# Row sums of the unit before the last: by ACT from the first score product, or by ones on TensorE

## The chip, the cores and the metric

The kernel runs on one core of one Trainium2 chip. The metric is the device time of one execution in microseconds (us). TensorE (PE, with its weight loads PEld), VectorE (DVE), ScalarE (ACT) and GpSimd (POOL) compute; SyncE (SP) issues almost all DMAs here.

## The reference, cut to what matters

A block of two parts over 2048 tokens of width 1024: an attention with a compressive memory (32 heads of width 32, four segments of 512 tokens, causal inside a segment), then an MLP. The change touches the softmax inside a segment:

```
logits = einsum("bhqd,bhkd->bhqk", qs, ks) * scale + mask
p      = softmax(logits, axis=-1)
a_dot  = einsum("bhqk,bhkd->bhqd", p, vs)
o      = g * a_mem + (1.0 - g) * a_dot
```

Afterwards `o @ wo` is added to the tokens, and layer norm, two dense layers with a GELU and a second addition follow. All in fp32; the dense products are made of three products of split operands (high x high, low x high, high x low).

## The kernel before, in words

The tokens are worked in two halves of 1024 tokens, each of two segments. In a half the attention runs over 16 **units**: eight groups `g` of four heads, and in each group the two segments `sl`. A unit's dense part (`dense`) projects keys, queries and values in 24 steps on TensorE, one step being one call of `mm3` (three matmuls). All that follows for the unit (`follow`) is written into a table of due times, in steps counted from the unit's start, and is performed between the dense steps of later units. So the score work of unit n lies beside the dense work of units n+1 and n+2. Behind the last unit the output product (`wo_first`) takes the place of the dense steps, with what is left of the table between its products. TensorE's order is the order of this table, fixed by hand; the order of the other engines comes from a scheduler with a cost model, with the dependences and buffers as limits.

What `follow` does for a unit, by the letters of the tables:

- `q` (`qk`, 16 calls: four heads, four row blocks): first score product into a bank of PSUM (`pqk`, one of four banks that the second product shares), then one DVE instruction (L663) that adds the mask, negates and gives the row maximum to `mx`. In an ordinary unit its output goes to an SBUF tile `sm` (four buffers), and ACT (L666) takes the exp of it only for the row sum, which goes to `mx` too.
- `x`, `y`, `z`: the maxima are split, transposed, and written over DRAM into two more rows of the query stack `qs`, so that the second product has the maximum already subtracted.
- `p` (`again`, 12 calls): second, transposed score product `psc`, exp by ACT into `pt` (L695), triangle by POOL (L697).
- `r`, `w` (`inverse`, `weigh`; ordinary units): reciprocal of the 16 columns of sums times the gate, a transpose `pw` on TensorE, a copy by ACT, a store to `r_dram` and four loads that spread it over `w`.
- `a`, `o` (`av`, `av_out`): product of `pt` with the values into `po`, times `w`, plus the memory part, then the split for the output product.

In the last group (`g == NG - 1`, so two units per half) `r` and `w` do nothing. L663 writes back into its PSUM bank and there is no exp for sums. Instead DVE adds the four `pt` blocks of a head (`sums`, L704 to L706), TensorE multiplies `pt` and the added block by `ones` (`den`, eight matmuls, in `av`), DVE takes the reciprocal of the whole 128x512 `den` (L739), and `av_out` has the gate as a per-row scalar.

The due times of the two last units differ from the ordinary ones: `LAST_FOLLOW` and `LAST_PACE` hold for the unit before the last, `END_FOLLOW` and `END_PACE` for the last. They have entries for `r` and `w` as well.

```
FOLLOW = dict(q=28.2, x=47.3, y=47.4, z=50.2, r=47.6, w=51.2, p=60.3, a=82.3, o=85.2)
PACE = dict(q=(4.7,1.2), p=(4.0, 1.3))
LAST_FOLLOW = dict(q=29.2, x=43.3, y=43.4, z=48.1, r=43.6, w=46.2, p=58.5, a=70.6, o=72.6)
LAST_PACE = dict(q=(3.5,0.9), p=(2.6,.85))
```

A pace `(a, b)` gives the steps from head to head and from block to block. The last unit's start is 24 steps behind that of the unit before it.

Of the kernel before, what the change touches and what calls it, by code (L numbers as in the profile page):

```python
# [10 lines left out]
F32 = mybir.dt.float32  # L11
# [6 lines left out]
P = 128  # L18
# [8 lines left out]
NG = 8  # L27
# [28 lines left out]
def build(tc, x, wq, wk, wv, wo, beta, w1, b1, w2, b2, out):  # L56
# [312 lines left out]
    def attention(half, first):  # L369
# [4 lines left out]
        def tmp(name):  # L374
            return ab.tile([P, 512], F32, tag="tmp", name=name, bufs=5)
# [262 lines left out]

        def follow(u):
            table, pace = (FOLLOW, PACE) if u["g"] < NG - 1 else ((LAST_FOLLOW, LAST_PACE), (END_FOLLOW, END_PACE))[u["s"] % 2]  # L640
            if u["g"] == NG - 1:
                for j in range(4):
                    u["at"](table["p"] + pace["p"][0] * j + LAG, partial(sums, u, j))
            for op, t in table.items():
                fn = fns[op]
                if op in pace:
                    a, b = pace[op]
                    for j in range(4):
                        for k, i in enumerate({"q": (0, 2, 1, 3), "p": (0, 1, 2)}[op]):
                            u["at"](t + a * j + b * k, partial(fn, u, j, i))  # L650
                else:
                    u["at"](t, partial(fn, u))

        def qk(u, j, i):
            if "mx" not in u:
                u["mx"] = ab.tile([P, 64], F32, name="mx", bufs=2)
            mx, n = u["mx"], P * (i + 1)
            pqk = psum.tile([P, 512], F32, tag="qk", name="pqk", bufs=4)
            one_small()
            nc.tensor.matmul(pqk[:, :n], u["qs"][0:96, j, i * P:(i + 1) * P], u["ks"][0:96, j, 0:n], start=True, stop=True)  # L660
            k = 4 * j + i
            pr = pqk if u["g"] == NG - 1 else ab.tile([P, 512], F32, name="sm", bufs=4)
            nc.vector.tensor_tensor_reduce(out=pr[:, :n], in0=pqk[:, :n], in1=mask[:, 512 - n:512], op0=ALU.add, op1=ALU.min,  # L663
                                           scale=-1.0, scalar=3.0e38, accum_out=mx[:, k:k + 1])
            if u["g"] < NG - 1:
                nc.scalar.activation(pr[:, :n], pr[:, :n], AF.Exp, bias=mx[:, k:k + 1], scale=-1.0, accum_out=mx[:, 16 + k:17 + k])  # L666

        def largest(u):
# [37 lines left out]
            SME.tensor_tensor(sm[:, 128:384], sm[:, 128:384], p2, op=ALU.add)  # L706

        def inverse(u):
            if u["g"] == NG - 1:
                return  # L710
            rs = u["rs"] = ab.tile([P, 32], F32, name="rs", bufs=2)
            nc.vector.reciprocal(rs[:, 0:16], u["mx"][:, 16:32])
            r4 = rs[:, 0:16].rearrange("p (h i) -> p h i", i=4)
            GTE.tensor_tensor(r4, r4, gate[:, 1, 4 * u["g"]:4 * u["g"] + 4].unsqueeze(2).to_broadcast([P, 4, 4]), op=ALU.mult)

        def weigh(u):
            n = acts["weighed"] = 1 - acts.get("weighed", 0)
            w = u["w"] = tmp("w") if u["g"] == NG - 1 and u["s"] % 2 else scr[n][:, 1]
            if u["g"] == NG - 1:
                return  # L720
            pw = ps_dense("pw")
            nc.tensor.transpose(pw[0:16, 0:P], u["rs"][:, 0:16], ident)
            nc.scalar.copy(w[0:16, 0:P], pw[0:16, 0:P])
            d = r_dram[n]
            BQ.dma_start(d, w[0:16, 0:P])
            for k in range(4):
                BQ.dma_start(w[32 * k:32 * k + 32, :],
                                  bass.AP(tensor=d.tensor, offset=d.offset + 512 * k, ap=[[0, DH], [1, 512]]))

        def av(u):  # L730
            u["po"] = psum.tile([P, 512], F32, tag="av", name="po", bufs=1)
            for jk in (0, 1, 3, 2):
                abreast([(u["po"][32 * j:32 * j + 32, P * jk:], u["v"]["vn"][:, j, jk, :], u["pt", jk][j], jk == 0, jk == 2)
                         for j in range(4)])
            if u["g"] == NG - 1:
                den = psum.tile([P, 512], F32, tag="qk", name="den", bufs=4)
                abreast([(den[32 * j:32 * j + 32, 0:P], ones, u["pt", 0][j][:, 0:P], True, True) for j in range(4)])
                abreast([(den[32 * j:32 * j + 32, P:], ones, u["sm"][j], True, True) for j in range(4)])
                nc.vector.reciprocal(u["w"], den)  # L739
            bursts()  # L740
# [5 lines left out]
        def av_out(u):  # L746
            w = u["w"]
            sl, g = u["s"] % 2, u["g"]
            home = w
            if kept(sl, g):  # L750
                if g % 2 == 0:
                    acts["home"] = {**acts.get("home", {}), sl: lnp.tile([P, D], F32, tag="ln", name="orr", bufs=4)}
                home = acts["orr", sl, g] = acts["home"][sl][:, 512 * (g % 2):512 * (g % 2) + 512]
            first = home if u["omt"] is None else w
            if g == NG - 1:
                nc.vector.scalar_tensor_tensor(w, u["po"], gcol, w, op0=ALU.mult, op1=ALU.mult)
            else:
                nc.vector.tensor_tensor(first, u["po"], w, op=ALU.mult)
            if u["omt"] is not None:
                w4, h4 = (t.rearrange("p (k c j) -> p k c j", k=4, c=4) for t in (w, home))  # L760
                nc.gpsimd.tensor_tensor(h4, w4, u["omt"].rearrange("p (c k j) -> p k c j", k=4, c=4), op=ALU.add)
            if u["g"] >= NG - 2:
                oh, ol = o_tiles(half, u["s"] % 2)
                split(None, w, oh[:, u["g"], :], ol[:, u["g"], :], hi_eng="scalar", lo_eng="vector")
            else:
                u["done"] = True
# [39 lines left out]
        prev = None  # L806
        for g in range(NG):
            for sl in range(2):
                u = {"g": g, "s": 2 * half + sl, "T": TIMES, "v": {}, "next": {}}
                d = dense(g, sl, ws, u)  # L810
                if prev is None:
                    interleave(d, acts.pop("ahead") if half else ln1(0, 1, aside=ws.pop("rest")), 1.1 if half else 1.6)
                    if first:
                        constants()
                    if "last" in acts:
                        acts.pop("last")
                else:
                    if g == NG - 1:
                        for n, fn in WO_AT[sl]:
                            acts["todo"].setdefault(acts["unit"] + 24 + n, []).append((0.9, n, fn))  # L820
                    with in_order(mybir.EngineType.PE, keep=False):
                        for _ in d:
                            pass
                prev = u
            ws = u["next"]
# [798 lines left out]
```

## Time and profile before

| | |
|---|---|
| median of 3 runs | 2139.03 us (2135.96 to 2140.15) |
| the profiled execution's own time | 2141.17 us |
| its span | 2139.5 us, 33505 instructions |
| TensorE busy | 2105.0 us, 98% |
| DVE, ACT, POOL busy | 1348.6 (63%), 1030.5 (48%), 853.9 us (40%) |
| DMA | 441.47 MB, mean 206 GB/s |

The shares are means over stages of quite different kinds. A view of waits names, for each group of instructions, what ended the idle time before it; a view in order of time gives start and duration of single instructions; "L666" is line 666 of the kernel. The last two units of the first half lie at about 364 to 414 us, those of the second at about 1159 to 1210 us; the output product follows each.

### The profile page before, as it was taken

The numbers are of one execution on the slowest core, as the hardware profiler recorded it, in microseconds if no ns is written. First come the engines' busy times: TensorE is split into PE (matmuls) and PEld (weight loads), VectorE is DVE, ScalarE is ACT, GpSimd is POOL, SyncE is SP. The second block draws the span as 40 slices with busy tenths as digits, with TensorE's granted clock in tenths as the row PEclk, the third lists the DMA queues.
The fourth block names the chain that finished last, engine by engine and source line by source line (L and its number), as shares of the span: only waits on it lengthen the run. The fifth ranks groups of instructions, "written<-read, shape, count | busy, mean of one in ns | idle before, by whom it ended". The sixth has DMA issues, their size and how long they took to land.

```text
span 2139.5 us, 33505 instructions
## 1 busy us (share of the span) xinstructions
PE 2105.0 (98%) x11157; PEld 1705.5 (80%) x11157; DVE 1348.6 (63%) x2679; ACT 1030.5 (48%) x2181; POOL 853.9 (40%) x937
## 2 busy tenths in 40 slices
PE   8999999999999999999999999999999999999999
PEld 6777877768888887877777778888888788888887
DVE  6666666676745556666666686655666675567653
ACT  5676677533633445667677434633443232323321
POOL 5333333432544423333333342534455544246340
PEclk9999999999999999999999999999999999999999
DMA  7777777834666557777778734665669774676762
GB/s 247 220 228 219 222 220 212 251 119 148 210 192 192 152 156 214 206 220 217 231 222 231 233 119 143 211 182 168 180 219 389 244 245 166 206 232 230 255 217 89
DMA packets 405783, 441.47 MB, mean 206 GB/s; under 512 B 36622, under 2 KB 270570, under 8 KB 405610
## 3 DMA queue, kind: packets, MB, share of 16 engines
q1 hardware_dynamic: 342442, 402.62, 60.9%
q10 hardware_dynamic: 63168, 36.71, 5.7%
q8 instruction: 88, 1.44, 0.3%
q14 instruction: 85, 0.70, 0.1%
HBM read 296.32 MB, written 142.90 MB: 205 GB/s over the span
## 4 chain that ended last, share of the span: by engine, by line
PE 88%; DMA 5%; DVE 3%; SPq 1%; POOL 1%; ACT 1%; issue 1%; ACTq 0%; POOLq 0%; DVEq 0%
PE po L1456 23%; PE bps L1060 10%; PE cps L1060 7%; PE dps L1060 7%; PE pqk L660 3%; PE psc L693 3%; PE po L463 3%; PE qps L140 3%; PE vps L140 3%; PE vps L141 3%; PE vps L142 3%; PE kps L140 3%; PE qps L141 2%; PE qps L142 2%; PE kps L141 2%; PE kps L142 2%
## 5 line engine op out<-in xcount | busy, mean ns | idle before, releaser
L663 DVE CUSTOM_DVE_ANT_0 sm<-pqk,mask 128x128 f32<-128x128 f32 x448 | 217.4, 488 | 205.5 <-PE pqk L660 194.4
L666 ACT ACTIVATE sm<-sm,mx 128x128 f32<-128x128 f32 x448 | 251.5, 562 | 175.3 <-DVE mx L663 172.5
L695 ACT ACTIVATE pt<-psc 128x512 f32<-128x512 f32 (+1 forms) x384 | 198.9, 521 | 94.6 <-PE psc L693 90.7
L697 POOL TENSOR_SCALAR_AFFINE_SELECT pt<-pt 128x128 f32<-128x128 f32 (+1 forms) x384 | 138.4, 366 | 253.8 <-ACT pt L695 250.6
L1466 DVE TENSOR_TENSOR c<-c,po 128x512 f32<-128x512 f32 x160 | 105.5, 684 | 154.5 <-PE po L1456 147.2
L660 PE MATMUL pqk<-ks,qs 96*128 96x128 f32 (+3 forms) x512 | 171.1, 335 | 11.9 <-DMA qs<-qs_dram 9.0
L693 PE MATMUL psc<-qs,ks 98*128 98x512 f32 (+3 forms) x512 | 139.5, 314 | 2.3 <-DVE mx L663 2.3
L1456 PE MATMUL po<-w2h,zh 128*128 128x512 f32 x378 | 120.9, 390 | 1.6 <-ACT zh L1395 1.2
L660 PEld LDWEIGHTS pqk<-ks,qs 96*128 96x128 f32 x512 | 96.6, 189 | 31.5 <-issue 9.4
L791 POOL TENSOR_TENSOR wl<-wr,wh 128x1024 fp32r<-128x1024 f32 x42 | 101.0, 2405 | 40.4 <-PE pqk L660 20.5
L693 PEld LDWEIGHTS psc<-qs,ks 98*128 98x128 f32 x512 | 95.9, 189 | 26.1 <-DVE mx L663 4.5
L1313 POOL TENSOR_TENSOR w2r<-w2r 128x512 f32<-128x512 f32 x54 | 84.6, 1576 | 72.8 <-DMA w2r<-in_B_w 50.2
L1060 PE MATMUL bps<-zh,sb 128*128 128x512 f32 x336 | 111.0, 391 | 0.0
L1060 PE MATMUL bps<-zh,sa 128*128 128x512 f32 x336 | 110.7, 390 | 0.0
L140 PE MATMUL kps<-yh,wh 128*128 128x512 f32 (+1 forms) x264 | 109.2, 414 | 0.0
L140 PE MATMUL qps<-yh,wh 128*128 128x512 f32 x256 | 107.8, 421 | 0.0
L140 PE MATMUL vps<-yh,wh 128*128 128x512 f32 x256 | 103.8, 405 | 0.0
L1456 PE MATMUL po<-w2h,hl 128*128 128x512 f32 x322 | 103.1, 390 | 0.4 <-DVE hl L1396 0.4
L141 PE MATMUL kps<-yl,wh 128*128 128x512 f32 (+1 forms) x264 | 102.9, 390 | 0.1
L142 PE MATMUL kps<-yh,wl 128*128 128x512 f32 (+1 forms) x264 | 102.5, 388 | 0.0
L1172 POOL TENSOR_TENSOR s<-r 128x512 f32<-128x512 f32 x28 | 44.1, 1574 | 142.8 <-DVE sa L1188 86.1
L141 PE MATMUL qps<-yl,wh 128*128 128x512 f32 x256 | 100.8, 394 | 0.0
(269 smaller groups left out, 5926.7 us busy)
## 6 DMA issues: line engine op xcount, KB each, us to landing
hr<-h_dram SPq DMA_DIRECT2D x112, 448.0 KB, 5.7
w2r<-in_B_w SPq DMA_DIRECT2D x122, 256.0 KB, 4.5
r<-in_B_w SPq DMA_DIRECT2D x56, 512.0 KB, 4.4
ks<-ks_dram SPq DMA_DIRECT2D x64, 384.0 KB, 3.9
qs<-qs_dram SPq DMA_DIRECT2D x64, 384.0 KB, 4.3
h_dram<-ht ACTq DMA_DIRECT2D x84, 256.0 KB, 3.6
ks_dram<-kh SPq DMA_DIRECT2D x64, 256.0 KB, 4.7
qs_dram<-qh SPq DMA_DIRECT2D x64, 256.0 KB, 3.0
```

What stands on the lines that cost most here:

```text
L140: nc.tensor.matmul(ps, ah, bh, start=first, stop=False)
L141: nc.tensor.matmul(ps, ah, bl, start=False, stop=False)
L142: acts["mm"] = nc.tensor.matmul(ps, al, bh, start=False, stop=last)
L660: nc.tensor.matmul(pqk[:, :n], u["qs"][0:96, j, i * P:(i + 1) * P], u["ks"][0:96, j, 0:n], start=True, stop=True)
L663: nc.vector.tensor_tensor_reduce(out=pr[:, :n], in0=pqk[:, :n], in1=mask[:, 512 - n:512], op0=ALU.add, op1=ALU.min, scale=-1.0, scalar=3.0 ...
L666: nc.scalar.activation(pr[:, :n], pr[:, :n], AF.Exp, bias=mx[:, k:k + 1], scale=-1.0, accum_out=mx[:, 16 + k:17 + k])
L693: nc.tensor.matmul(ps[:, o:o + m], u["ks"][:, j, jk * P:(jk + 1) * P], u["qs"][:, j, P * jk:], start=True, stop=True)
L695: nc.scalar.activation(pt, ps[:, :w], AF.Exp)
L697: nc.gpsimd.affine_select(d, d, pattern=[[1, P]] if len(groups[n]) == 1 else [[0, 2], [1, P]], compare_op=ALU.is_ge, fill=0.0, base=0, cha ...
L1060: nc.tensor.matmul(ps, x_[:, c, :], y_[:, c, :], start=first and c == 0 and n == 0, stop=last and c == 3 and n == 2, skip_group_check=True)
L1456: nc.tensor.matmul(ps, x_[:, k], y_[k], start=opens and k == 0 and i == 0, stop=closes and k == self.KP - 1 and i == 2, skip_group_check=True)
L1466: nc.vector.tensor_tensor(o, o, ps, op=ALU.subtract if name == "4" else ALU.add)
```

## The change

The ones on TensorE remain for one unit per half only, the last (`"last": g == NG - 1 and sl == 1`). The unit before it (`g == NG - 1`, `sl == 0`) does what the ordinary units do: L663 writes to `sm`, ACT makes the row sums with 16 exps, `inverse` and `weigh` do their work at the times that `LAST_FOLLOW` has for `r` and `w`, and `sums`, `den` and the wide reciprocal fall away for it. No due time is changed.

```diff
         def follow(u):
...
-            if u["g"] == NG - 1:
+            if u["last"]:
                 for j in range(4):
                     u["at"](table["p"] + pace["p"][0] * j + LAG, partial(sums, u, j))
...
-            pr = pqk if u["g"] == NG - 1 else ab.tile([P, 512], F32, name="sm", bufs=4)
+            pr = pqk if u["last"] else ab.tile([P, 512], F32, name="sm", bufs=4)
...
-            if u["g"] < NG - 1:
+            if not u["last"]:
                 nc.scalar.activation(pr[:, :n], pr[:, :n], AF.Exp, bias=mx[:, k:k + 1], scale=-1.0, accum_out=mx[:, 16 + k:17 + k])
...
         def inverse(u):
-            if u["g"] == NG - 1:
+            if u["last"]:
                 return
...
-            w = u["w"] = tmp("w") if u["g"] == NG - 1 and u["s"] % 2 else scr[n][:, 1]
-            if u["g"] == NG - 1:
+            w = u["w"] = tmp("w") if u["last"] else scr[n][:, 1]
+            if u["last"]:
                 return
...
-            if u["g"] == NG - 1:
+            if u["last"]:
                 den = psum.tile([P, 512], F32, tag="qk", name="den", bufs=4)
...
-            if g == NG - 1:
+            if u["last"]:
                 nc.vector.scalar_tensor_tensor(w, u["po"], gcol, w, op0=ALU.mult, op1=ALU.mult)
...
-                u = {"g": g, "s": 2 * half + sl, "T": TIMES, "v": {}, "next": {}}
+                u = {"g": g, "s": 2 * half + sl, "T": TIMES, "v": {}, "next": {}, "last": g == NG - 1 and sl == 1}
```

## The prediction

> **What bounds the kernel now.** I read the page first, then the chain of waits on TensorE for the whole run and for the ends of the two halves, then the order of time around the last two units of each half.
>
> ```profile
> PE 2105.0 (98%) x11157; PEld 1705.5 (80%) x11157; DVE 1348.6 (63%) x2679; ACT 1030.5 (48%) x2181; POOL 853.9 (40%) x937
> ```
>
> TensorE is busy for 2105.0 of 2139.5 us, so only two things move the time: TensorE work that is added or taken away, and the few places where TensorE stands still. ACT at 48% says nothing yet, because that is a mean over stages. The places where TensorE waits:
>
> ```profile
> PE pqk L660 <- DMA qs<-qs_dram: 9.0, 7, 2.4
> PE psc L693 <- DVE mx L663: 2.3, 3, 1.3
> ...
> PE pw L722 <- DVE rs L714: 1.4, 2, 0.7
> ```
>
> The reader should see three kinds of wait. The longest single one (2.4 us) is for the query stack of the last unit; 2.3 us go to score banks that DVE frees late; and `pw`, the transpose of the row-sum inverses, is waited for in the ordinary units too, but only twice with an idle TensorE, 1.4 us in all. The change brings two more `pw` transposes, so this last row is the one to watch.
>
> How full are the other engines where the unit before the last runs its first score product? The columns are the stretch, its length, then busy time of PE, PEld, DVE, ACT and POOL, the granted clock, and DMA.
>
> ```profile
> 395.00:411.00 16.00, 15.61 (x126) 11.76 (x125) 13.05 (x42) 8.71 (x15) 6.12 (x10) 1.00 0.84 284
> 1189.30:1207.10 17.80, 16.74 (x132) 12.58 (x131) 12.59 (x46) 7.40 (x13) 7.43 (x11) 1.00 0.73 241
> 432.30:435.70 3.40, 3.40 (x16) 1.50 (x20) 0.36 (x2) 0.00 (x0) 0.00 (x0) 0.54 0.40 148
> ```
>
> The first two rows are that stretch in the first and the second half: ACT has 8.71 us of work in 16.0 us, and 7.40 us in 17.8 us. The third row lies just behind the 2.4 us wait: the granted clock is 0.54 for 3.4 us, so that wait costs about 3.4 x 0.46 = 1.6 us more than itself.
>
> **The change part by part.**
>
> *Removed on TensorE: the products with ones of the unit before the last.* The two views in order of time, one per half:
>
> ```profile
> 458.69 0.40 PE L463 MATMUL den<-pt,ones 128*32 128x128 f32 x8
> 458.91 0.94 PE L463 MATMUL den<-sm,ones 128*32 128x384 f32 x8
> 459.77 0.50 PE L140 MATMUL pwo<-wh,oh 128*128 128x512 f32 x1
> ```
>
> ```profile
> 1251.95 0.40 PE L463 MATMUL den<-pt,ones 128*32 128x128 f32 x8
> 1252.17 1.50 PE L463 MATMUL den<-sm,ones 128*32 128x384 f32 x8
> 1253.61 0.50 PE L140 MATMUL pwo<-wh,oh 128*128 128x512 f32 x1
> ```
>
> From the first `den` to the next product: 459.77 - 458.69 = 1.08 us, and 1253.61 - 1251.95 = 1.66 us. All of it is on TensorE's own path, nothing hides it, and it goes: **-2.7 us**. This is the surest term.
>
> *Removed on DVE: the adds of `sums` (four triples per unit) and the full-width reciprocal.*
>
> ```profile
> L704 DVE TENSOR_TENSOR sm<-pt,pt x16: 541/552/659, 444.6 to 1270.8; 128x384 f32<-128x384 f32 x16
> L739 DVE RECIPROCAL scl<-den x2: 3358/3358/3358, 459.9 to 1253.7; 128x512 f32<-128x512 f32 x2
> ```
>
> Per half that is 3.36 us of reciprocal and four times 0.55 us plus two smaller adds each. They lie in the first part of the output product, where TensorE has its own work queued; the only TensorE waits on DVE there are the two `psc` waits of the last unit (1.3 us the longest, 2.3 us over three), and those come before the first of the adds is reached. Ends: 0, or -2.1 if a freer DVE also took those two waits away. I take 0. `scalar_tensor_tensor` in `av_out` becomes `tensor_tensor`, one for one, off the path: 0.
>
> *Added on ACT: sixteen exps per half that only make row sums.* What one costs is in the unit before that, grouped by shape, and in order of time for one of them:
>
> ```profile
> L666 ACT ACTIVATE sm<-sm,mx 128x512 f32<-128x512 f32 x5 | 3.6, 724 | 1.0 <-DVE mx L663 1.0
> L666 ACT ACTIVATION_READ_ACCUMULATOR sm<-sm,mx 128x1 f32 x17 | 3.2, 188 | 0.0
> L666 ACT ACTIVATE sm<-sm,mx 128x384 f32<-128x384 f32 x4 | 2.5, 617 | 1.6 <-DVE mx L663 1.4
> L666 ACT ACTIVATE sm<-sm,mx 128x256 f32<-128x256 f32 x4 | 2.0, 504 | 2.9 <-DVE mx L663 2.9
> ...
> L666 ACT ACTIVATE sm<-sm,mx 128x128 f32<-128x128 f32 x4 | 1.6, 394 | 1.1 <-DVE mx L663 1.1
> ```
>
> ```profile
> 388.12 0.72 ACT L666 ACTIVATE sm<-sm,mx 128x512 f32<-128x512 f32 x1 [0.31 <-DVE mx L663]
> 388.75 0.18 ACT L666 ACTIVATION_READ_ACCUMULATOR sm<-sm,mx 128x1 f32 x1
> ```
>
> The read of the accumulator overlaps the exp's end by 0.09 us, so it adds 0.1 us. One head is 0.72 + 0.62 + 0.50 + 0.39 + 4 x 0.1 = 2.64 us, four heads 10.5 us. First half: 8.7 + 10.5 = 19.2 us of ACT work in a stretch of 16.0 us, 3.2 us too much. Second half: 7.4 + 10.5 = 17.9 us in 17.8 us, full to the brim. And ACT cannot use all of it, since DVE hands over no scores for a while. The same stretch shows it as idle time before the cast of `oh`, first half and second half:
>
> ```profile
> L115 ACT CAST oh<-scl 128x512 fp32r<-128x512 f32 x1 | 0.6, 620 | 2.1 <-DVE scl L758 2.1
> ```
>
> ```profile
> L115 ACT CAST oh<-scl 128x512 fp32r<-128x512 f32 x1 | 0.6, 621 | 6.4 <-POOL scl L761 6.4
> ```
>
> Backlog fills part of these gaps. I leave 1 us unfilled in the first half and 4 us in the second (6.4 less the exps of the first head and a half, 1.5 x 2.64 = 4.0, is 2.4, and some of the other short gaps stay). ACT then finishes the last exp at 411.0 + 3.2 + 1 = 415.2 us and at 1207.1 + 0.1 + 4 = 1211.2 us.
>
> *Added on TensorE's path: the `pw` transpose, at the place that `LAST_FOLLOW` gives it (w=46.2), not moved by the change.* That is step 22 of the last unit, just ahead of these score products:
>
> ```profile
> 413.26 0.28 PE L693 MATMUL psc<-qs,ks 98*128 98x256 f32 x1
> ```
>
> ```profile
> 1209.51 0.28 PE L693 MATMUL psc<-qs,ks 98*128 98x256 f32 x1
> ```
>
> Behind the last exp still come two small DVE instructions and the hand-overs:
>
> ```profile
> L714 DVE TENSOR_TENSOR rs<-rs,gate x28: 163/177/1996, 59.6 to 1184.2; 128x16 f32<-128x16 f32 x28
> ```
>
> I allow 0.5 us for both. So `rs` is ready at 415.7 and 1211.7, and TensorE, which runs in order, waits 2.4 and 2.2 us at `pw`: **+4.6 us**. Queued behind it are the rest of the value product and the first output product, so nothing on TensorE covers the wait. Ends: 0.7 us per wait, the longest in the ordinary units' row, if ACT keeps up as there (which gives +1.4, or 0 if it hides entirely); and 4 us per half if none of the gaps is filled. I take the middle because the ordinary units spread their four heads over 4.7 steps each and leave 3.6 steps between inverse and transpose, while this unit has 3.5 and 2.6. The transpose itself takes a slot of under 0.1 us: 0.
>
> *Added on SP: five small transfers per half.* One store of the inverses and four loads that spread them, as in 28 units now:
>
> ```profile
> L725 SPq DMA_DIRECT2D r_dram<-scl x14: 328/328/433, 62.2 to 1164.2; - x14
> ...
> DMA to landing us min/median/max: 1.3/1.4/3.3
> ```
>
> ```profile
> L727 SPq DMA_DIRECT2D scl<-r_dram x56: 313/420/1878, 66.5 to 1167.2; - x56
> ```
>
> 0.33 + 4 x 0.42 = 2.0 us of SP time, and a wait of 1.4 us for the store to land, during which SP, being in order, holds whatever is behind: the weight pieces of the output product, `vlast`, and the `ks` and `qs` fetch of the last unit. This is the dangerous neighbour, for that `qs` fetch is what TensorE waits for at 432 us:
>
> ```profile
> 418.42 0.39 ACT L695 ACTIVATE pt<-psc 128x256 f32<-128x256 f32 x1 [0.27 <-PE psc L693]
> 418.70 1.13 ACT L115 CAST wth<-wr 128x512 fp32r<-128x512 f32 x2
> ```
>
> ```profile
> 421.93 0.38 SPq L867 DMA_DIRECT2D wr<-in_A_wo  x1
> 422.50 1.75 SPq L392 DMA_DIRECT2D vlast<-turn_dram  x4
> 424.29 0.43 SPq L437 DMA_DIRECT2D ks<-ks_dram  x1
> 424.77 0.45 SPq L437 DMA_DIRECT2D qs<-qs_dram  x1
> ```
>
> ACT casts `wth` behind the score exp, POOL subtracts, SP may then load `wr`, and only then come `vlast`, `ks` and `qs`. If ACT is 2 us late, this chain is 2 us late too, so the new wait at `pw` is not swallowed by the old wait for `qs`; both stay. That is why I let the 4.6 us through whole. For the five transfers themselves: 0 if they fall into SP's pause before 421.93, 2.0 us per half if they stand ahead of `qs`. I take 0, because SP is only waiting there.
>
> *DVE's mask-and-maximum now writes `sm` in SBUF instead of its PSUM bank:* same instruction, same bank release, 0. But it may not run more than four exps ahead of ACT (`sm` has four buffers), which turns an ACT backlog into a TensorE wait somewhat earlier; that is the same wait, not a second one.
>
> **Sum:** -2.7 + 4.6 + 0 = **+1.9 us**. The profiled execution took 2141.17 us (span 2139.5), 2.1 us above the median of the three runs; the sum on the median 2139.03 gives **2141 us**. About 0.2% (4.3 us) is what a measurement of this kernel can tell from no change.
>
> **A rule weighed.** The 3.4 us at half clock stand behind a wait of 2.4 us. The Trainium skill, "TensorE: Matmul & The Clock Gate", section "Part 1: The HAM clock gate", has the clock halved only after an idle window of about 3.4 us; by that rule the new waits of 2.4 and 2.2 us would cost nothing more and the sum stays +1.9, while by the row each could cost another 1.6 us and the sum would be +5.1. The trace speaks against a plain reading of the rule, since a 2.4 us wait was enough.
>
> **The rivals.**
>
> *ACT keeps up.* For it: 28 units do the same today and wait at `pw` for 1.4 us in all. Against: their pace is slower. Then only the products with ones count: -2.7 us, 2136.3. Chance 0.13, inside 0.2%.
>
> *Faster: the new wait takes the place of the wait for `qs`.* If the `wth` cast and the SP chain do not move, TensorE comes 2 us later to 432 us and finds `qs` nearly there; the old wait and the slow clock behind it (1.6 us in each half) go. That is -2.7 + 4.6 - 4.6 - 3.2 = -5.9 us, 2133. It decides if the chain to `qs` slips by under 0.5 us. Against: ACT stands in that chain. Chance 0.17.
>
> *Slower: each new wait also halves the clock, or the five transfers push `qs` back.* The first gives +1.9 + 3.2 = +5.1 us, the second up to +1.9 + 4.0 = +5.9, both +9, so 2144 to 2148. It decides from a wait of some 2.2 us in one piece. For it: my two waits are of just that size. Against: the backlog may spread over several short waits. Chance 0.28.
>
> **How the numbers follow.** The forecast (+1.9, own range 0 to +4) has 0.42. Within 0.2%: 0.42 + 0.13 = 0.55; faster 0.17; slower 0.28. The range reaches from the faster rival to the far end of the slower one, 2134 to 2148.
>
> **What would show it.** Right: `den` twice instead of four times; L666 with 480 instead of 448; in the wait view a new row of TensorE at `pw` of about 2 us in each half, near 413 and 1210; the `qs` wait still there. Wrong: no wait at `pw` (ACT kept up); a `qs` wait under 1 us with a full clock behind it (faster rival); more stretches at half clock, or a `qs` wait above 4 us (slower rival).

## Result and profile after

The changed kernel takes 2150.56 us (median of 4 runs, 2150.43 to 2153.28) against 2139.03 us of the kernel before measured beside it: ratio 1.0055, 95% interval 1.004 to 1.0071. One run of the kernel before, of 2594.94 us, was in a slower state of the chip and is left out, as such runs are in every ratio below. The change costs some 11 to 12 us. Forecast were 2141 us and a range of 2134 to 2148; the time lies above the range, on the side of the slower rival and beyond the 2148 that it was given.

The profiled execution took 2150.44 us (span 2148.7). The page's first line and the row of the exps, which answer to those of before:

```profile
PE 2104.3 (98%) x11127; PEld 1704.8 (79%) x11127; DVE 1322.9 (62%) x2657; ACT 1046.1 (49%) x2247; POOL 849.0 (40%) x937
...
L666 ACT ACTIVATE sm<-sm,mx 128x128 f32<-128x128 f32 x480 | 269.3, 562 | 185.1 <-DVE mx L663 179.5
```

The change did what it says: 480 exps, 25.7 us less of DVE, 15.6 us more of ACT, TensorE work all but equal. The loss is idle time, so the next view is TensorE's waits for the whole run (line, what ended the wait, total us, times, longest):

```profile
PE pqk L660 <- DMA qs<-qs_dram: 17.4, 5, 6.3
...
PE pw L722 <- DVE rs L714: 4.9, 4, 2.2
...
PE psc L693 <- ACT pt L695: 0.7, 1, 0.7
```

The wait for `qs` was 9.0 us in all with 2.4 the longest; now it is 17.4 and 6.3. The wait at `pw` that the prediction was about is there, 2.2 us in the first half and 1.3 in the second. Stretch by stretch (the end of each half, a row per wait, first half and second half):

```profile
PE pqk L660 <- DMA qs<-qs_dram: 6.3, 1, 6.3
```

```profile
PE pqk L660 <- DMA qs<-qs_dram: 5.9, 1, 5.9
```

The same two waits were 2.4 and 2.3 us before. With each of them comes a stretch in which TensorE is granted half its clock, now twice as long. It starts before the wait ends: in the changed kernel at 435.9 us, where `qs` comes at 438.33, so that some 4.5 of the 6.9 us are worked at half clock. The columns are the stretch, its length, busy time of PE, PEld, DVE, ACT and POOL, the clock, and DMA:

```profile
435.90:442.80 6.90, 4.47 (x20) 1.84 (x24) 0.36 (x2) 0.00 (x0) 0.00 (x0) 0.51 0.70 222
1238.00:1244.90 6.90, 4.24 (x20) 1.77 (x24) 0.36 (x2) 0.00 (x0) 0.00 (x0) 0.51 0.59 183
```

Before, it was 3.41 us in each half:

```profile
1227.30:1230.71 3.41, 3.41 (x18) 0.80 (x20) 0.03 (x1) 0.00 (x0) 0.00 (x0) 0.50 0.20 70
432.00:435.41 3.41, 3.11 (x12) 1.45 (x16) 0.36 (x2) 0.00 (x0) 0.00 (x0) 0.50 0.49 183
```

That gives an account of the two ends of a half, from the last key product of the last unit to the last wide reciprocal: together 173.8 us before, 184.7 after, +11.0. TensorE's idle time in them is +10.7 of it: waits for `qs` +7.5, at `pw` +3.5, short waits -0.3. Its busy time is only +0.3: -2.7 for the ones, +1.1 for the slow clock (busy 8.7 instead of 6.5 us in these rows, half of the difference), and +1.9 that I assign to nothing in particular (two transposes are in it, and ends of matmuls are modelled). The two profiled executions as wholes differ by 9.2 us, so the rest of the changed one was 1.8 us shorter. Outside these two stretches the order of instructions on every engine is that of before.

Why is `qs` late? SP's order of time, first half, before (the rows ahead of those that the prediction shows) and after:

```profile
412.09 0.34 SPq L677 DMA_DIRECT2D m_dram<-mt  x1
412.53 0.40 SPq L867 DMA_DIRECT2D wr<-in_A_wo  x1
...
416.89 0.46 SPq L387 DMA_DIRECT2D turn_dram<-sch  x1
```

```profile
412.47 0.34 SPq L677 DMA_DIRECT2D m_dram<-mt  x1
415.89 0.40 SPq L867 DMA_DIRECT2D wr<-in_A_wo  x1
...
417.38 0.40 SPq L725 DMA_DIRECT2D r_dram<-scl  x1
...
419.70 0.46 SPq L387 DMA_DIRECT2D turn_dram<-sch  x1
423.73 1.72 SPq L727 DMA_DIRECT2D scl<-r_dram  x4
...
428.74 1.89 SPq L392 DMA_DIRECT2D vlast<-turn_dram  x4
430.73 0.38 SPq L437 DMA_DIRECT2D ks<-ks_dram  x1
431.15 0.45 SPq L437 DMA_DIRECT2D qs<-qs_dram  x1
```

From the store of `mt` to the fetch of `qs` SP took 424.77 - 412.09 = 12.7 us before and 431.15 - 412.47 = 18.7 us after. The reader should see two holds. The first stands right behind `mt`: the load of `wr` comes 3.4 us late. The second stands ahead of the four loads: SP's own waits, after, with the landing of the store beside them (its size, and the us from issue to landing):

```profile
SPq L727 <- DMA r_dram<-scl: 3.5, 1, 3.5
SPq L867 <- POOL pt L697: 3.2, 1, 3.2
```

```profile
r_dram<-scl SPq DMA_DIRECT2D x1, 8.0 KB, 6.3
```

The store of 8 KB took 6.3 us to land in this place; the prediction had 1.4, the median of the other units. The first hold is POOL's subtraction for the piece of `wo` that `wr` is to replace. It waits for ACT's cast, and the cast stood behind the added exps: before and after,

```profile
406.55 1.05 ACT L115 CAST wh<-wr 128x1024 fp32r<-128x1024 f32 x1 [0.26 <-PE qps L141]
```

```profile
412.37 1.07 ACT L115 CAST wh<-wr 128x1024 fp32r<-128x1024 f32 x1
413.31 0.75 ACT L666 ACTIVATE sm<-sm,mx 128x512 f32<-128x512 f32 x1
413.52 2.35 POOL L116 TENSOR_TENSOR wl<-wr,wh 128x1024 fp32r<-128x1024 f32 x1 [0.54 <-ACT wh L115]
413.93 0.22 ACT L666 ACTIVATION_READ_ACCUMULATOR sm<-sm,mx 128x1 f32 x1
414.18 0.25 DVE L712 RECIPROCAL rs<-mx 128x16 f32<-128x16 f32 x1 [1.74 <-ACT sm L666]
414.47 1.43 DVE L714 TENSOR_TENSOR rs<-rs,gate 128x16 f32<-128x16 f32 x1
415.95 0.28 PE L722 MATMUL pw<-ident,rs 128*16 128x128 f32 x1 [2.18 <-DVE rs L714]
```

(The wait view names POOL's last short instruction, L697; what ends at 415.87, 0.02 us ahead of the load, is the subtraction of L116.) So there are two suspects for the late `qs`: **the transfers** (SP held by the landing of the store, and the loads themselves) and **ACT's exps** (casts of `wo` late, and behind them POOL, SP and the pieces that TensorE needs).

### The profile page after: what moved, and what is told of

Its sections match the earlier page's. It is cut to its first block, busy times and chain, and to the rows that moved or that the text cites. A ratio compares the mean times of both kernels' runs of the same rounds, so it can differ in the third digit from the quotient of the medians.

```text
span 2148.7 us, 33500 instructions
## 1 busy us (share of the span) xinstructions
PE 2104.3 (98%) x11127; PEld 1704.8 (79%) x11127; DVE 1322.9 (62%) x2657; ACT 1046.1 (49%) x2247; POOL 849.0 (40%) x937
## 4 chain that ended last, share of the span: by engine, by line
PE 90%; DMA 3%; ACT 2%; DVE 2%; SPq 1%; POOL 1%; issue 1%; DVEq 0%; POOLq 0%; ACTq 0%
PE po L1456 23%; PE bps L1060 11%; PE cps L1060 7%; PE dps L1060 7%; PE pqk L660 3%; PE psc L693 3%; PE po L463 3%; PE qps L140 3%; PE kps L140 3%; PE vps L140 3%; PE qps L141 2%; PE qps L142 2%; PE vps L141 2%; PE vps L142 2%; PE kps L141 2%; PE kps L142 2%
## 5 line engine op out<-in xcount | busy, mean ns | idle before, releaser
L663 DVE CUSTOM_DVE_ANT_0 sm<-pqk,mask 128x128 f32<-128x128 f32 x480 | 231.6, 488 | 208.1 <-PE pqk L660 199.0
L666 ACT ACTIVATE sm<-sm,mx 128x128 f32<-128x128 f32 x480 | 269.3, 562 | 185.1 <-DVE mx L663 179.5
L697 POOL TENSOR_SCALAR_AFFINE_SELECT pt<-pt 128x128 f32<-128x128 f32 (+1 forms) x384 | 135.8, 358 | 263.2 <-ACT pt L695 258.2
L660 PE MATMUL pqk<-ks,qs 96*128 96x128 f32 (+3 forms) x512 | 171.5, 336 | 19.6 <-DMA qs<-qs_dram 17.4
L141 PE MATMUL vps<-yl,wh 128*128 128x512 f32 x256 | 100.7, 393 | 0.0
```

Source lines behind the costliest of these rows:

```text
L141: nc.tensor.matmul(ps, ah, bl, start=False, stop=False)
L697: nc.gpsimd.affine_select(d, d, pattern=[[1, P]] if len(groups[n]) == 1 else [[0, 2], [1, P]], compare_op=ALU.is_ge, fill=0.0, base=0, cha ...
```

## The experiments

Theory A at the outset: the transfers carry the loss, since they stand ahead of the `qs` fetch on an in-order queue. Rival B: ACT's backlog carries it. Differences in us below are ratio less one, times 2139 us.

**The four loads moved behind the `qs` fetch** (all else as changed):

```diff
+        def spread(u):          # the four loads, taken out of weigh, called at due time d
-LAST_FOLLOW = dict(... r=43.6, w=46.2, p=58.5, ...)
+LAST_FOLLOW = dict(... r=43.6, w=46.2, d=56.0, p=58.5, ...)
```

> The changed kernel, except that the four loads from r_dram of the unit before the last are issued 9.8 steps later (a due time of their own, 56.0), so that in SP's order they stand behind the ks and qs fetch of the last unit; store, transpose and exps as in the change. Theory A (SP, in order, is held by the wait for the landing of the r_dram store and then issues four loads ahead of qs): the qs fetch goes out about 4.4 us earlier than the changed kernel's 431.15 us, TensorE's wait for qs falls from 6.3 and 5.9 us to 2 to 3 us, the stretch at half clock from 6.8 to 3.4 us per half, time 2140 to 2143 us against 2150.5. Theory B (the sixteen exps make ACT late, and with it the casts of wo, the wr loads and so qs): nothing moves by more than 1 us, qs waits stay over 5 us, time 2149 to 2151.

Measured 2144.29 us, ratio 1.0021 [1.0009, 1.0033], 7 us less than the changed kernel. The two waits for `qs` fall to 2.2 and 1.7 us; the waits at `pw` stay at 2.2 and 1.3. By the medians the place of the loads is worth more than half of the loss. Here, and not in the changed kernel, the clock halves behind the wait at `pw`: the two rows are that wait and the 4 us from just ahead of its end.

```profile
PE pw L722 <- DVE rs L714: 2.2, 1, 2.2
```

```profile
417.00:421.00 4.00, 3.54 (x10) 2.90 (x11) 2.03 (x3) 1.68 (x3) 1.53 (x5) 0.57 0.54 171
```

**The sixteen exps alone** (kernel before, the exps added for that unit, their sums unused; ones stay on TensorE, no transpose, no transfers):

```diff
-            pr = pqk if u["g"] == NG - 1 else ab.tile([P, 512], F32, name="sm", bufs=4)
+            pr = pqk if u["g"] == NG - 1 and u["s"] % 2 else ab.tile([P, 512], F32, name="sm", bufs=4)
-            if u["g"] < NG - 1:
+            if u["g"] < NG - 1 or u["s"] % 2 == 0:
```

> The kernel before, with only the sixteen exps for row sums added to the unit before the last (their sums go unused; ones on TensorE, the wide reciprocal and all transfers stay as before; L663 writes to sm as in the change). Theory A: ACT's backlog costs no wait at pw, since there is none; the wr loads come some 2 us later, so the qs wait is 2.4 to 4.5 us and the time 2139 to 2144 us. Theory B: the qs waits are 5 to 6 us and the clock is halved for 6.8 us per half as in the changed kernel, time 2149 to 2153 us.

Measured 2144.56 us, 1.0028 [1.0018, 1.0038]: +6.0 us with nothing but exps. There is no `pw` to wait at, and TensorE waits under other names (first half):

```profile
PE pwo L140 <- ACT wth L115: 1.6, 1, 1.6
PE pqk L660 <- DMA qs<-qs_dram: 1.3, 1, 1.3
PE pwo L141 <- POOL wtl L116: 0.9, 1, 0.9
```

TensorE waits for the second pieces of `wo`, which ACT casts late. In the second half it waits 0.8 and 0.6 us for them, where it had not waited before, and 2.5 us for `qs`. From `mt` to `qs` SP took 15.6 us instead of 12.7. The time lies just above what theory A allowed (2139 to 2144 us), far below theory B; the waits for `qs` are at or below the low end of A's. So exps that no `pw` waits for do cost, but not all of the loss.

**The change without the exps** (its inverses are made from what is there, the maxima):

```diff
-            if not u["last"]:
+            if u["g"] < NG - 1:
                 nc.scalar.activation(pr[:, :n], ...)
-            nc.vector.reciprocal(rs[:, 0:16], u["mx"][:, 16:32])
+            nc.vector.reciprocal(rs[:, 0:16], u["mx"][:, 16:32] if u["g"] < NG - 1 else u["mx"][:, 0:16])
```

> The changed kernel without the sixteen exps in the unit before the last: its weights are made from the maxima instead of the row sums, so that transpose, copy, store and loads stay where they are. Theory A: no wait at pw, but SP is still held for the landing of the r_dram store; the store goes out 2 us earlier, so part of the wait falls into SP's own pause: qs wait 3 to 5 us, time 2138 to 2146 us. Theory B: the qs wait falls back to 2.4 us or less and, with ones on TensorE gone, time 2135 to 2138 us. If the wait for qs stays at 6 us, the exps have no part in it.

Measured 2144.76 us, 1.0030 [1.0018, 1.0041]: +6.4 us with transpose and transfers alone, although the ones (2.7 us) are gone. No wait at `pw`; waits for `qs` of 3.5 and 5.3 us; SP held by the store as in the changed kernel:

```profile
SPq L727 <- DMA r_dram<-scl: 3.0, 1, 3.0
```

From `mt` to `qs` SP took 15.1 us. So exps alone give +2.9 us on that queue, transfers alone +2.4, both +6.0; and in the median times +6.0, +6.4 and +11.8. By the medians the two causes add, within intervals of 2 us and more; the profiled executions, compared at the end of this section, show a part that needs both. Neither A nor B is the whole.

**The transpose and its transfers later** (`r=45.6, w=50.2` instead of 43.6 and 46.2):

> The changed kernel with two due times of LAST_FOLLOW moved: r from 43.6 to 45.6 and w from 46.2 to 50.2, so the pw transpose stands 4 steps (some 4 us) later on TensorE; store and loads follow it, and in SP's order the loads still stand ahead of the ks and qs fetch of the last unit. Theory A: the waits at pw (2.2 and 1.3 us) go, but TensorE then only waits longer for qs, since SP is still held by the landing of the store, now ahead of vlast: time 2148 to 2153 us. A third theory C (the wait at pw itself is what delays everything behind it, the qs chain with it): both waits shrink, time 2139 to 2144 us. Theory B: pw wait gone, qs wait as it is or longer by 2 us, time 2149 to 2151 us.

Measured 2148.19 us, 1.0048 [1.0031, 1.0065]. The wait at `pw` is gone, but the loads are still ahead of `qs`, its waits stay at 5.4 and 4.4 us, and 1.6 us come up at `wth`. The term that the prediction was built on is not what makes most of the loss.

**Both: transpose later, loads behind the fetch** (the edits of the first and the fourth run together):

> The changed kernel with the pw transpose 4 steps later and the four loads behind the qs fetch, but the order of the other loads left as it was. No wait at pw, qs wait as with exps alone (1.3 and 2.5 us there). If the parts add up, it is the kernel with only the exps (2144.6 us) less the ones on TensorE (2.7 us): 2140 to 2144 us. If it stays at 2147 us or more, there is a cost in the change that none of the parts so far has shown.

Measured 2142.8 us, 1.0009 [0.9997, 1.0022]: no wait at `pw`, `qs` at most 2.3 us, and the time that of the kernel before, though 2.7 us of TensorE work are gone.

**The `qs` fetch first.** In five runs the `ks` and `qs` fetch of the last unit gets an earlier due time and the pieces 3 and 4 of `wo` are asked for later, so the fetch stands ahead of `wr` and `vlast` on SP:

```diff
-                at(T["kf"] + 7 * p, partial(stack_fetch, "ks", p))
+                at(T["kf"] + (6.0 if g == NG - 1 and sl == 1 else 7) * p, partial(stack_fetch, "ks", p))
-                at(T["qf"] + 6.5 * p, partial(stack_fetch, "qs", p))
+                at(T["qf"] + (5.0 if g == NG - 1 and sl == 1 else 6.5) * p, partial(stack_fetch, "qs", p))
...
-        ahead(1)
-            ... else ahead(2) if (t, i) == (0, 5) else None)
+            ... else ahead(1) if (t, i) == (1, 1) else ahead(2) if (t, i) == (1, 5) else None)
```

In the kernel before:

> The kernel before with only the order of loads altered behind the last unit: the ks and qs fetch of its last two heads is due one step earlier (27 instead of 28) and the third and fourth pieces of wo are asked for later, so that in SP's order this fetch stands ahead of vlast and of the wr load that waits for POOL. It asks how much the qs wait is worth by itself. If the wait and the half clock behind it are on the path: both go in both halves, 2 x (2.4 + 1.7) = 8 us, time 2129 to 2133 us. If DMA bandwidth rather than SP's order is the limit, the wait moves to the wr pieces and the time stays at 2136 to 2140 us.

Measured 2135.02 us, 0.9970 [0.9958, 0.9983]: 6.4 us faster than the kernel before, the wait for `qs` at the ends 0.3 us at most, no half clock there. By the ratio that is 2132.6 of 2139 us, inside the first forecast, by the plain median between the two: the wait was on the path.

In the changed kernel:

> The changed kernel with the same order of loads (ks and qs fetch one step earlier, the third and fourth wo pieces later). The store to r_dram and its four loads still stand ahead of the fetch in SP's order. Theory A (SP held by the landing of the store): the fetch goes out earlier by what the wr load took, but still behind the loads: qs wait 1 to 3 us, time 2139 to 2145 us, so 8 to 14 us above the kernel before with this order. Theory B (ACT's lateness alone, through the wo casts): the fetch no longer hangs on those casts, so the qs wait is gone and the time 2131 to 2136 us.

Measured 2145.82 us, 1.0023 [1.0012, 1.0033]. The fetch gains about as much as in the kernel before, so the cost of the change stays at 11 us: the loads are held until 423.48 us and the fetch behind them goes at 427.28 us. By the ratio, 2143.9 of 2139 us, the time lies in theory A's range, far from B's.

With transpose late, loads behind and fetch first:

> The changed kernel with the same order of loads, the pw transpose 4 steps later (r 45.6, w 50.2) and the four r_dram loads at a due time of their own (56) behind the qs fetch: every wait that the change brought should be gone, and what is left is its plain balance, ones on TensorE (-2.7 us) against sixteen exps on ACT. Theory A (exps cost only through waits that other work was made to share): 0 to 4 us below the kernel before with this order, 2127 to 2132 us. Rival D (the exps themselves cost TensorE some 5 us, through late wo casts and late second-score exps): 1 to 4 us above it, 2133 to 2137 us.

Measured 2140.46 us, 0.9995 [0.9983, 1.0006]: no wait at `pw`, none for `qs` at the ends, yet 5 us above the same kernel without the change, and above what either theory had. What is left at the end of the first half are the pieces of `wo`, and a stretch at half clock behind them:

```profile
PE pwo L140 <- ACT wth L115: 1.5, 1, 1.5
...
PE pwo L141 <- POOL wtl L116: 0.9, 1, 0.9
```

**The cast of the second `wo` pieces on DVE** instead of ACT, in that last kernel. If the exps cost through these casts, it goes:

```diff
-            wts[0, k] = wo_halves(wraw[k], k, wo_home())
+            wts[0, k] = home = wo_home()
+            split(None, wraw[k], home[0], home[1], "vector" if k == 1 else "scalar", "gpsimd" if k % 2 else "vector")
```

> The changed kernel with the late turn and the early qs fetch of the run at 2140.5 us, and the cast of the second wo pieces moved from ACT to DVE. Theory D (the sixteen exps cost through the wo casts that stand behind them on ACT): TensorE's waits for wth and wtl (1.5 and 0.9 us the longest) shrink below 0.7 us, the stretch at half clock near 422 us goes, time 2134 to 2138 us. Rival (the exps cost through something else, DVE being as late as ACT): waits of the same size under other names, 2139 to 2143 us.

Measured 2131.04 us, 0.9955 [0.9942, 0.9968]. All that TensorE waits for at the end of the first half:

```profile
PE psc L693 <- DVE mx L663: 1.5, 2, 1.3
PE pqk L660 <- DVE scl L384: 0.3, 1, 0.3
PE pwo L141 <- POOL wtl L116: 0.3, 1, 0.3
PE pqk L660 <- DVE mx L663: 0.2, 1, 0.2
```

The wait for `wth` and the half clock are gone, and 0.3 us are left of the wait for `wtl`. The time is below the expected 2134 to 2138.

**Its twin without the change** (kernel before, fetch first, cast on DVE) tells whether that is the change's or the cast's own gain:

> The kernel before with the early qs fetch (2135.0 us) and with the cast of the second wo pieces on DVE instead of ACT: the twin of the run at 2131.0 us without the change itself. Theory D (the exps cost only through ACT; with the cast on DVE that cost is gone and the ones on TensorE are the only difference): 2133 to 2136 us, that is 2 to 4 us above 2131.0, the 2.7 us of the products with ones. Rival (moving the cast is a gain of its own, whatever ACT has to do): 2126 to 2131 us, equal to or below the twin.

Measured 2128.91 us against 2135.82 of the kernel before beside it: 0.9964 [0.995, 0.9978]. (The kernel before took 2135.82 us beside this run and beside two others, some 4 us less than beside the rest, so ratios are compared: 0.9964 of 2140 is 2132.) By the ratios the twin is 2 us above, as theory D had it; but the intervals overlap, and the plain median lies in the rival's range, so the times alone do not decide. The moved cast gives 0.9970 to 0.9964 without the exps, some 1 us, and 0.9995 to 0.9955 with them, some 9 us; these two gains differ by more than their intervals allow. So, in this order of loads, the exps do cost through the cast behind them. The two ends in the profiled executions agree: with the cast moved TensorE is idle there for 4.2 us with the change and 4.1 without, and busy for 158.0 and 160.0 us. What is left of the change is 2.0 us less work, near the 2.7 of the ones.

**The cast moved in the changed kernel, and nothing else:**

> The changed kernel with the cast of the second wo pieces on DVE and nothing else: the turn and the loads stay where the change put them, ahead of the qs fetch. Theory (two separate costs: ACT's backlog 6 us through the late casts, the held queue 6 us): the cast part goes, the hold stays, 2143 to 2147 us, qs waits of 3 to 6 us. Rival (one cost, the late cast being what makes the queue late): qs waits of 2.5 us or less, 2136 to 2141 us.

Measured 2147.39 us against 2135.82, 1.0050 [1.0034, 1.0067]. The waits at `pw` go in both halves, and the second half's end gets 3.6 us shorter. But the loads still stand ahead of `qs`, whose waits are 5.7 and 4.8 us, and in this execution another wait of 3.2 us for an earlier `qs` stands in the first half. The waits for `qs` are those of two separate costs, as the theory had it, and not of one; the time is not, since the gain of about 1 us is within the interval and less than the 3 to 7 expected. The new wait hides some 3 us of a gain in this execution, and why it came is not known. So what the cast is worth in the changed kernel as it stands is not shown.

**Is it SP's wait for the landing, or the loads?** First, the loads read the other `r_dram` tile:

```diff
             BQ.dma_start(d, w[0:16, 0:P])
+            if u["g"] == NG - 1:
+                d = r_dram[1 - n]
```

> The changed kernel with one edit: for the unit before the last, the four loads that spread the inverses read the other r_dram tile, written by an earlier unit, so the output heads of that unit are weighed with another unit's inverses. The store and the four loads are still issued at the same place, ahead of the qs fetch; only the wait of SP for the fresh store to land is gone (3.5 us in half 1, about as much in half 2). Theory A (SP held by the landing of the store makes up most of what the transfers cost): the qs fetch is issued about 3.5 us earlier than in the changed kernel, the two waits for qs shrink from 6.3 and 5.9 us to 2.5 to 4 us, time 2143 to 2147 us. Rival (what costs is the issue and the traffic of the five transfers, wherever they land): qs waits stay above 5 us, time 2149 to 2152 us.

Measured 2154.03 us, 1.0067 [1.005, 1.0085]. This run does not answer, since SP is held by the same store as before: the loads overwrite the rows of `w` that the store is still reading.

```profile
SPq L729 <- DMA r_dram<-scl: 4.6, 1, 4.6
```

So the store was given other rows to read as well:

```diff
-            BQ.dma_start(d, w[0:16, 0:P])
+            BQ.dma_start(d, w[0:16, 0:P] if u["g"] < NG - 1 else ident[0:16, :])
+            if u["g"] == NG - 1:
+                d = r_dram[1 - n]
```

> The changed kernel with one edit: for the unit before the last, the store takes its rows from a constant tile and the four loads read the r_dram tile that an earlier unit has written, so nothing waits for this store and the output heads of that unit are weighed with another unit's inverses. Unlike in the run before it of this kind, the loads do not overwrite the rows that the store reads, either. Three of the four loads are still issued ahead of the qs fetch and wait for ACT's copy of the inverses, the fourth and the store go earlier. Theory A (the wait of SP for the fresh store is 3.5 us per half of the 6.4 us by which the qs fetch came late): the qs waits shrink from 6.3 and 5.9 us to 2.5 to 4 us, time 2143 to 2147 us. Rival (the queue is late because of ACT and the landing of other transfers, and the hold only overlaps that): qs waits above 5 us, time 2148 to 2152 us.

Measured 2147.82 us against 2135.82, 1.0054 [1.0039, 1.0068]. The hold on `r_dram` is gone and the four loads are out by 419.2 us, yet the fetch goes at 430.29 us, 17.4 us behind `mt`: only 1.3 of the 6.0 us come back. SP's waits and order show what took its place:

```profile
SPq L869 <- POOL pt L697: 3.2, 1, 3.2
SPq L392 <- DMA turn_dram<-sch: 2.3, 1, 2.3
SPq L682 <- DMA ks<-ks_dram: 1.3, 1, 1.3
SPq L682 <- DMA qs<-qs_dram: 1.0, 1, 1.0
```

```profile
420.73 0.33 SPq L387 DMA_DIRECT2D turn_dram<-sch  x1
...
428.01 1.76 SPq L392 DMA_DIRECT2D vlast<-turn_dram  x4
429.87 0.38 SPq L437 DMA_DIRECT2D ks<-ks_dram  x1
430.29 1.44 SPq L437 DMA_DIRECT2D qs<-qs_dram  x1
```

The next pair of store and load, `turn_dram` and `vlast`, now waits for its own landing, 7.3 us from issue to the first load. Ahead of it the two small loads into `qs` (L682) waited for the landing of the `ks` and the `qs` fetch, the eighth DMA ahead of each. The waits for `qs` at the ends did fall, to 2.6 and 1.9 us, and the two ends take 178.4 instead of 184.7 us in the profiled executions; the medians do not show it (the rest of that execution is 5 us longer, with a wait of 4.8 us for a `qs` near 835 us). The run is not a clean one either: with the other `r_dram` tile, here and in the run before it, TensorE waits twice for 1.4 us at `pm` (L558), which it does at the ends of no other run, and comes that much later to `qs`. So theory A has its waits and not its time: removing the wait for this landing alone buys nothing that the medians show.

**The five transfers where nobody waits** (kernel before, a store and four loads of the same size, behind the `qs` fetch):

> The kernel before with one addition: in each half five transfers of the size of the change's (a store of 8 KB and four spreading loads into the last unit's weights, which that unit overwrites) are issued on SP behind the qs fetch (due 56.0), where nothing waits for them. Theory A (transfers cost only through what they hold up): 2138 to 2141 us, the qs waits at 432 and 1227 us within 0.5 us of 2.4 and of the second half's, the wait near 835 us about 2.2 us. Rival (the five transfers make the start of the second half later, whatever their place, since the kernels that have them wait 3.2 to 3.8 us near 835 us and those without 1.9 to 2.7): that wait 3.2 us or more, time 2141 to 2144 us.

Measured 2137.22 us, 0.9990 [0.9981, 0.9998]; wait near 835 us 2.1 us. Five transfers per half cost nothing in this place. It is their place that costs.

**The two ends side by side.** The medians hold the whole execution, and outside the two ends a profiled execution took 1960.7 to 1973.0 us, whatever the kernel. So the table has the ends alone (last key product of the last unit to last wide reciprocal, both halves, one profiled execution of each kernel):

| Kernel | ratio | both ends, us | TensorE idle in them, us |
|---|---|---|---|
| before | 1 | 173.8 | 10.4 |
| changed | 1.0055 | 184.7 | 21.2 |
| loads behind the fetch | 1.0021 | 173.5 | 12.1 |
| exps alone | 1.0028 | 178.6 | 13.0 |
| change without exps | 1.0030 | 174.9 | 13.8 |
| transpose and transfers later | 1.0048 | 181.9 | 18.2 |
| transpose later, loads behind | 1.0009 | 173.2 | 11.3 |
| before, fetch first | 0.9970 | 166.4 | 5.9 |
| changed, fetch first | 1.0023 | 175.7 | 14.2 |
| fetch first, transpose late, loads behind | 0.9995 | 168.9 | 9.1 |
| the same, cast on DVE | 0.9955 | 162.2 | 4.2 |
| before, fetch first, cast on DVE | 0.9964 | 164.1 | 4.1 |
| changed, cast on DVE | 1.0050 | 181.5 | 17.2 |
| other `r_dram` tile | 1.0067 | 185.2 | 22.5 |
| other tile and constant rows | 1.0054 | 178.4 | 16.0 |
| before, idle transfers | 0.9990 | 171.9 | 9.8 |

Three things can be read from it. With the loads behind the fetch all of the 11 us at the ends are gone; what that kernel still loses in its median lies elsewhere. Idle time at the ends grows by 2.6 us with the exps alone, by 3.4 with transpose and transfers alone, and by 10.7 with both: the 3.5 us at `pw` are there only when the exps are late and the transpose waits for them. And the cast moved to DVE takes 4.9 us of idle time away with the exps, 1.8 without.

## Why the prediction was wrong, point by point

- **Ones off TensorE, -2.7.** The products are gone as counted. What that buys was not isolated beyond the 2.0 us of TensorE work between the two kernels with fetch first and cast on DVE.
- **The wait at `pw`, +4.6.** Right in kind and nearly in size: 2.2 and 1.3 us, 3.5 in all, against 2.4 and 2.2. But the way there had two errors that cancelled in the first half. ACT was done about a us earlier than I had it (414.15, not 415.2 us), and the hand-over took 1.8 us, not 0.5: the small multiply of `rs` (L714), 0.18 us by the median of its row, took 1.43 us and ended at 415.90, 0.03 us behind POOL's subtraction. The row's own maximum of 1.996 us was the warning.
- **The five transfers, 0. This is the step that failed.** "I take 0, because SP is only waiting there" has three faults. The store was priced at the median landing of 1.4 us, where this queue was full: 6.3. The loads did not fall into a pause but made one, 3.5 us, with `qs` behind it. And the far end of the rival, 2.0 us per half, was the issue time of the five transfers alone; the fetch went 6.0 us later behind `mt`, and 2.4 us with transpose and transfers alone. The first run bears it out: loads behind the fetch, 7 us back.
- **ACT's late chain to `qs`.** I wrote that "if ACT is 2 us late, this chain is 2 us late too" and used it only to keep the old wait of `qs` alive. It had to be charged as well: the exps alone put the fetch 2.9 us back and cost 6.0 us, with waits for `wth` and `wtl` in both halves. A wait at `pw` plus a later chain is two costs; I counted one. That it goes through the cast is shown by the pair with the cast on DVE, for the order with the fetch first; in the changed kernel itself it was not shown.
- **DVE, 0.** Nearly so. In the second half TensorE waited 0.8 us at `pwo` for a DVE addition to `ht` (L891 before) that stood behind the adds, a wait which the prediction did not list. All five profiled kernels that keep the ones of the unit before the last have it, none of the eleven others has.
- **The rule weighed.** The Trainium skill, "TensorE: Matmul & The Clock Gate", section "Part 1: The HAM clock gate", has half clock only after an idle window of about 3.4 us. The traces do not need so much: 2.4 us of waiting were enough in the kernel before. In the changed kernel the 4 us behind both waits at `pw` were granted 1.00, as the rule would have it; with the loads moved, the same 2.2 us came with 0.57. The traces show what it goes by. Within one execution the stretches at half clock start whole multiples of 3.41 us apart (with the loads moved at 417.28, 437.76 and 837.12 us), and each lasts 3.41 or 6.83 us unless the program ends first. So time can be cut into slots of 3.41 us, and what counts is TensorE's idle time within one slot. The wait at `pw` in the changed kernel fell across the edge of two slots, the same wait with the loads moved into one (first fence changed, second with the loads moved; slot by slot, columns as above):

```profile
412.07:415.48 3.41, 1.70 (x9) 1.08 (x7) 1.60 (x4) 3.33 (x7) 2.37 (x2) 1.00 0.21 57
415.48:418.89 3.41, 2.94 (x14) 2.49 (x15) 2.02 (x3) 1.77 (x4) 1.54 (x5) 1.00 0.45 124
```

```profile
413.87:417.28 3.41, 1.35 (x7) 0.83 (x5) 1.64 (x3) 3.04 (x7) 2.66 (x2) 1.00 0.16 36
417.28:420.69 3.41, 3.23 (x9) 2.66 (x10) 1.44 (x3) 1.68 (x3) 1.25 (x5) 0.50 0.54 165
```

Idle were 1.71 us of the slot at 412.07, and 2.06 of the one at 413.87. Over the sixteen profiles (from 40 us on), a slot at full clock with 2.0 us or more of idle time was followed by half clock every time, one with less than 1.7 never; between the two both occurred. So whether a wait of about 2 us costs clock depends on where it falls, and the prediction had no way to know.

- **Rivals.** "The five transfers push `qs` back" was named with 0.28 and is what came in part, but its bound was too low: the rival's two cases together were given +9, by half clock behind `pw`, which did not come, and by 4.0 us for the transfers. ACT's late chain was in neither.

Two things stay open. Why taking away the hold on `r_dram` moves the median so little when the trace of the ends shows 6 us: the rest of an execution varies by several us, and a single profile does not settle it. And why the first `qs` of the second half, near 835 us, is waited for 3.2 to 4.8 us in ten of the eleven kernels that have the change's weights (2.7 in the other) and 1.8 to 2.6 us in the five without; the idle transfers rule out the transfers as such, the rest was not tried. It may be where kernels with the loads behind the fetch still lose what their ends no longer show; with the loads moved, 3.8 us of waiting and 6.83 us at half clock stand there against 2.2 and 3.41 before.

## What to carry to other kernels

Price a store that is read back on the same in-order queue by its landing time in that place, with that backlog, not by the median of the run; and charge everything behind it. When work is put on an engine with spare time, list what stands behind it there (here casts that feed POOL, SP and TensorE in turn) before looking at the one wait that the new work itself brings. And look for the transfer that is on the path already: fetching `qs` earlier and moving one cast gave 0.996 of the time, without the change, or with it once its transpose and loads were moved too.

## What the runs showed of the hardware

- A store of 8 KB landed in 1.4 us as a rule and in 6.3 us with loads of 512, 384 and 384 KB issued on the same queue in the 1.5 us before it; one of 256 KB took 7.3 us until its first reader could go. Here the landing went with what stood ahead of the store on its queue.
- A DVE multiply of 128x16 took 1.43 and 1.46 us instead of 0.18 while a POOL subtraction ran, and ended 0.03 us after it, in both halves (415.90 and 1218.88 us), and 0.04 us after it with the loads moved. The reciprocal just ahead of it, with one input, took 0.25 us beside the same subtraction; its median is 0.21. The Trainium skill, "SBUF — State Buffer", section "Summary: rules for kernel authors", says that a DVE operation with two SBUF inputs is blocked for the whole of a GpSimd operation that reads SBUF and came first; the rows agree.
- TensorE's half clock came in slots of 3.41 us on a fixed grid within an execution: always behind a slot at full clock with 2.0 us or more of idle time, never behind one with less than 1.7 us (sixteen profiles).
